# Attention over 32 memories and a SwiGLU block: memory values multiplied into the gate and value weights, attention with memories on partitions, engines ordered by the program

## The chip, the cores and the metric

The kernel runs on one core of one Trainium2 chip. The time is the device time of one execution in microseconds. The kernel before has a median of 433.32 us over three runs (431.91 to 434.16). A core has TensorE (matrix products into PSUM), VectorE, ScalarE (functions and copies), GpSimd (called POOL in the profile) and SyncE (SP, which issues transfers); 16 DMA engines move data between HBM and the on-chip memory SBUF. GpSimd issues transfers too, and those alone can change the type on the way.

## The reference

There are 8 batches, 8 heads, 576 positions, 64 numbers per head and 32 memories. For each batch and head, with `a` a softmax over the 32 memories of `phi`:

```python
k_m = einsum('bhsm,bhsd->bhmd', a, k)      # 32 memory keys of 64 numbers
v_m = einsum('bhsm,bhsd->bhmd', a, v)      # 32 memory values
```

`a` is `exp(phi - max over positions)` divided by its sum over positions; the sum runs over the 576 positions, for each memory. Then

```python
attn = softmax(q @ k_m.T / sqrt(64))       # over the 32 memories
x    = attn @ v_m                          # heads side by side: 4608 tokens x 512
out  = (silu(x @ w_gate) * (x @ w_val)) @ w_out
```

`w_gate` and `w_val` are 512 x 1536, `w_out` is 1536 x 512. Inputs and output are float32; the products are made in bfloat16 with float32 sums.

For one batch, `x @ w_gate` is the sum over heads of `attn_h @ (v_m_h @ w_gate_h)`, where `w_gate_h` are the 64 rows that belong to the head. The inner product has 8 x 32 = 256 rows, and so the product with `attn` has a contraction of 256 where `x @ w_gate` has 512.

## The kernel before, in words

A position s of a head lies on partition p = s // 6, column j = s % 6, with 96 partitions; the transposes put the 576 positions of a batch in the order (j, p), and the output's view `out_r` undoes it.

`attention_pair(b, a)` treats two heads. It loads phi by SyncE (L101) and q, k, v by GpSimd with a cast to bfloat16 (L105, L109, L113), six pieces of 256 bytes for each partition and head, adds columns of ones (L117), and takes exp of phi on ScalarE (L120). Six matmuls (L129, 258 columns: k and v of two heads and two columns of ones) give the memories with their sums. VectorE takes the reciprocals (L142), ScalarE scales into the two blocks of a block-diagonal `t_bkv` (L145), whose zeros GpSimd writes (L125). TensorE transposes the keys and q (L153, L155), VectorE copies them to SBUF (L162), six matmuls make the scores with positions on partitions (L166). ScalarE takes exp (L175), VectorE sums over memories, inverts and multiplies (L177 to L181). After the `yield` comes the back half: transposes of the weights of attention (L191), their copy (L198), and the product with the memory values (L202, L206), which ScalarE copies into X (L209, L210): 128 features of a pair of heads on partitions, 4608 tokens.

`ffn_chunk(c)` treats 512 tokens. For each of 12 blocks of 128 of the 1536 hidden features it runs four matmuls for the gate (L234) and four for the value (L242), each with 128 rows of contraction and 512 columns; ScalarE takes Tanh of half the gate (L250), VectorE makes two products (L252, L256). Then four tiles of 128 tokens: 12 matmuls each (L265), a copy on ScalarE (L273) and the transfer out (L275).

Weights come by SyncE as float32 and are cast by VectorE (L76, L77). The loops run over batches and pairs of heads; the back half of a pair is issued after the front half of the next, and a chunk as soon as its tokens are there. The order on each engine is not the order of the program: a planner places instructions by priority and by when their inputs are due, so that the profile shows attention of the next batch between the matmuls of a chunk.

Of the kernel before, what the change touches and what calls it, by code (L numbers as in the profile page):

```python
# [10 lines left out]
FP32 = mybir.dt.float32  # L12
# [4 lines left out]
def kernel(  # L17
# [10 lines left out]
):  # L28
    nc = tc.nc
    AF = mybir.ActivationFunctionType  # L30
    ALU = mybir.AluOpType
    AXL = mybir.AxisListType
# [4 lines left out]
    NT = out.shape[0]  # L37
    P, J = 96, 6
    KVC = 2 * (2 * D + 1)
    sm_scale = 1.0 / math.sqrt(D)  # L40

    n_pairs = H // 2
    N_CI = DM // 128
    N_FJ = DF // 128
    TCH = 512
    N_TC = NT // TCH

    consts = ctx.enter_context(tc.tile_pool(name="consts", bufs=1))
    bridge = ctx.enter_context(tc.tile_pool(name="bridge", bufs=1))
    wpool = ctx.enter_context(tc.tile_pool(name="wpool", bufs=1))  # L50
    wstage = ctx.enter_context(tc.tile_pool(name="wstage", bufs=3))

    att_sb = ctx.enter_context(tc.tile_pool(name="att_sb", bufs=3))
    ffn_sb = ctx.enter_context(tc.tile_pool(name="ffn_sb", bufs=2))
    ps = ctx.enter_context(tc.tile_pool(name="ps", bufs=1, space=bass.MemoryType.PSUM))

    ident = consts.tile([128, 128], BF16, tag="ident", name="ident")
    make_identity(nc, ident)

    Xs = [bridge.tile([128, NT], BF16, tag=f"X{i}", name=f"X{i}") for i in range(4)]  # L60

    WG = [wpool.tile([128, DF], BF16, tag=f"WG{i}", name=f"WG{i}") for i in range(N_CI)]
    WV = [wpool.tile([128, DF], BF16, tag=f"WV{i}", name=f"WV{i}") for i in range(N_CI)]
    WO = [wpool.tile([128, DM], BF16, tag=f"WO{i}", name=f"WO{i}") for i in range(N_FJ)]

    weight_jobs = []

    def _make_wjob(dst, src_ap, big, idx):
        def run():
            st = wstage.tile(  # L70
                [128, DF if big else DM],
                FP32,
                tag="wst_big" if big else "wst_small",
                name=f"wst{idx}",
            )
            nc.sync.dma_start(out=st, in_=src_ap)  # L76
            nc.vector.tensor_copy(out=dst, in_=st)  # L77

        return run

    _wi = 0
    for i in range(N_CI):
        weight_jobs.append(_make_wjob(WG[i], moe_w_gate[128 * i:128 * (i + 1), :], True, _wi))
        _wi += 1
    for i in range(N_CI):
        weight_jobs.append(_make_wjob(WV[i], moe_w_val[128 * i:128 * (i + 1), :], True, _wi))
        _wi += 1
# [263 lines left out]
```

## Time and profile before

| what | value |
|---|---|
| median of the runs | 433.32 us |
| span of the profiled execution | 430.0 us |
| between span and median | 3.3 us |
| TensorE busy | 377.2 us (88%) |
| VectorE busy | 229.4 us (53%) |
| ScalarE busy | 159.3 us (37%) |
| GpSimd busy | 155.3 us (36%) |
| moved by DMA | 38.16 MB, of it 14.17 MB by GpSimd's queue |
| first matmul | at 20.70 us |

No time of its own is given for the profiled execution beside its span; the median is that of three runs without a profile. The page divides the span into 40 equal slices and gives each engine a digit of tenths. Groups of instructions are given as busy time, mean time of one and idle time before them. Matmuls are pipelined, so the mean of one is longer than the distance between two; the distance is read from the timeline.

### The profile page before, as it was taken

How to read it: one execution, taken by the hardware profiler on the slowest of the kernel's cores; microseconds unless marked ns; L12 is line 12 of the kernel's file. 1: busy time of each engine (PE TensorE's matmuls, PEld its weight loads, DVE VectorE, ACT ScalarE, POOL GpSimd, SP SyncE). 2: the span in 40 equal slices, each digit the busy share in tenths (PEclk: the TensorE clock that was granted, in tenths of full speed). 3: DMA queues.
4: the chain of work that ended last, by engine and by line, in shares of the span. 5: the costliest groups of instructions: out<-in, count | busy, mean ns of one | idle time of the engine just before them, and what ended most of it. 6: DMA issues, size and time to landing. Idle time of an engine off the chain costs nothing.

```text
span 430.0 us, 6163 instructions
## 1 busy us (share of the span) xinstructions
PE 377.2 (88%) x2160; PEld 180.0 (42%) x2160; DVE 229.4 (53%) x460; ACT 159.3 (37%) x337; POOL 155.3 (36%) x262
## 2 busy tenths in 40 slices
PE   0036667999999999999999999999999999999995
PEld 0023333444444444444444444444444444444442
DVE  1136534780678067807780777077707770871760
ACT  1012333532553255335533553355334533332321
POOL 7068558750763076307621772176300000000000
PEclk9999955999999999999999999999999999999999
DMA  9999999992996299639963995398630003003003
GB/s 253 320 239 112 230 161 102 99 69 75 110 95 41 75 116 91 41 84 103 93 40 98 102 89 34 94 94 51 41 98 0 3 2 98 0 2 98 2 1 96
DMA packets 129502, 38.16 MB, mean 89 GB/s; under 512 B 116160, under 2 KB 122304, under 8 KB 129472
## 3 DMA queue, kind: packets, MB, share of 16 engines
q0 software_dynamic: 113664, 14.17, 53.7%
q1 hardware_dynamic: 15808, 23.60, 19.5%
q8 instruction: 17, 0.28, 0.3%
q14 instruction: 13, 0.11, 0.1%
HBM read 42.47 MB, written 9.44 MB: 121 GB/s over the span
## 4 chain that ended last, share of the span: by engine, by line
PE 74%; DMA 13%; POOL 6%; ACT 3%; issue 3%; DVE 0%; POOLq 0%; ACTq 0%; DVEq 0%
PE p_oo L265 22%; PE p_g L234 20%; PE p_v L242 19%; DMA t_kvb<-in_v_dram 13%; PE p_kvS L129 4%; PE p_aT L191 2%; POOL t_kvb L109 2%; POOL t_qb L105 2%; PE p_kqT L155 2%; PE p_sc L166 2%; PE p_o L202 2%; ACT t_T L250 1%; ACT t_bkv L145 1%; POOL t_kvb L113 1%; PE p_kqT L153 1%
## 5 line engine op out<-in xcount | busy, mean ns | idle before, releaser
L234 PE MATMUL p_g<-X,WG 128*128 128x512 bf16 x432 | 121.1, 385 | 0.6 <-ACT X L209 0.6
L242 PE MATMUL p_v<-X,WV 128*128 128x512 bf16 x432 | 119.3, 386 | 0.8 <-DVE t_B L252 0.8
L250 ACT ACTIVATE t_T<-p_g 128x512 bf16<-128x512 f32 x108 | 64.3, 595 | 88.2 <-PE p_g L234 82.7
L252 DVE SCALAR_TENSOR_TENSOR t_B<-t_T,p_v 128x512 bf16<-128x512 bf16 x108 | 74.0, 685 | 41.9 <-PE p_v L242 32.8
L265 PE MATMUL p_oo<-WO,t_h 128*128 128x512 bf16 x432 | 94.7, 379 | 0.0
L109 POOL DMA_DIRECT2D t_kvb<-in_k_dram x64 | 46.7, 730 | 80.8 <-PE p_kvS L129 75.1
L256 DVE SCALAR_TENSOR_TENSOR t_h<-t_B,p_g 128x512 bf16<-128x512 bf16 x108 | 73.2, 678 | 2.3
L265 PEld LDWEIGHTS <-t_h 128*128 128x128 bf16 x432 | 42.3, 98 | 50.9
L242 PEld LDWEIGHTS <-WV 128*128 128x128 bf16 x432 | 40.5, 99 | 48.2 <-issue 4.8
L234 PEld LDWEIGHTS <-WG 128*128 128x128 bf16 x432 | 38.3, 98 | 46.2 <-issue 8.9
L142 DVE RECIPROCAL t_rS<-p_kvS 32x1 f32<-32x1 f32 x64 | 10.1, 157 | 84.0 <-PE p_kvS L129 72.4
L129 PE MATMUL p_kvS<-t_kvb,t_ephi 96*64 96x258 bf16 x192 | 31.1, 304 | 24.7 <-POOL t_kvb L117 24.6
L273 ACT COPY t_o<-p_oo 128x512 f32<-128x512 f32 x36 | 21.1, 585 | 80.2 <-PE p_oo L265 80.2
L105 POOL DMA_DIRECT2D t_qb<-in_q_dram x64 | 48.5, 761 | 2.6 <-issue 2.6
L113 POOL DMA_DIRECT2D t_kvb<-in_v_dram x64 | 47.4, 741 | 2.9 <-issue 1.5
L145 ACT ACTIVATE t_bkv<-p_kvS,t_rS 32x128 bf16<-32x128 f32 x64 | 22.6, 353 | 37.6 <-DVE t_rS L142 32.7
L129 PEld LDWEIGHTS <-t_ephi 96*64 96x64 bf16 x192 | 20.5, 119 | 35.2 <-issue 33.5
L117 POOL MEMSET t_kvb<- 96x12 bf16 x32 | 4.8, 149 | 63.8 <-DMA t_kvb<-in_v_dram 63.7
L175 ACT ACTIVATE t_att<-p_sc 96x384 bf16<-96x384 f32 x32 | 15.5, 484 | 32.0 <-PE p_sc L166 31.9
L209 ACT CAST X<-p_o 128x512 bf16<-128x512 f32 x32 | 18.7, 584 | 18.8 <-PE p_o L206 18.8
L198 DVE COPY t_aT<-p_aT 64x576 bf16<-64x576 bf16 x32 | 14.3, 446 | 21.3 <-PE p_aT L191 21.3
L162 DVE COPY t_kqT<-p_kqT 128x640 bf16<-128x640 bf16 x32 | 15.7, 489 | 17.3 <-PE p_kqT L155 17.3
(28 smaller groups left out, 204.5 us busy)
## 6 DMA issues: line engine op xcount, KB each, us to landing
t_phi<-in_phi_dram SPq DMA_DIRECT2D x64, 72.0 KB, 2.8
t_qb<-in_q_dram POOLq DMA_DIRECT2D x64, 72.0 KB, 3.4
t_kvb<-in_k_dram POOLq DMA_DIRECT2D x64, 72.0 KB, 3.5
t_kvb<-in_v_dram POOLq DMA_DIRECT2D x64, 72.0 KB, 3.6
out_dram<-t_o SPq DMA_DIRECT2D x24, 192.0 KB, 2.3
wst<-in_moe_w_gate_dram SPq DMA_DIRECT2D x4, 768.0 KB, 7.1
wst<-in_moe_w_val_dram SPq DMA_DIRECT2D x4, 768.0 KB, 7.1
wst<-in_moe_w_out_dram SPq DMA_DIRECT2D x12, 256.0 KB, 5.3
```

What stands on the lines that cost most here:

```text
L105: nc.gpsimd.dma_start(out=t_qb[:, :, hh, :], in_=q[b, h].rearrange("(p j) d -> p j d", p=P),)
L109: nc.gpsimd.dma_start(out=kvb_heads[:, hh, :, 0:D], in_=k[b, h].rearrange("(p j) d -> p j d", p=P),)
L113: nc.gpsimd.dma_start(out=kvb_heads[:, hh, :, D:2 * D], in_=v[b, h].rearrange("(p j) d -> p j d", p=P),)
L129: nc.tensor.matmul(p_kvS, lhsT=t_ephi[:, j], rhs=t_kvb[:, j], start=(j == 0), stop=(j == J - 1),)
L145: nc.scalar.activation(out=bkv_blk[rows, :, D * hh:D * hh + D], in_=p_kvS[rows, off:off + 2 * D], func=AF.Copy, scale=t_rS[rows, :],)
L234: nc.tensor.matmul(p_g, lhsT=WG[i][:, 128 * jf:128 * (jf + 1)], rhs=Xs[i][:, cols], start=(i == 0), stop=(i == N_CI - 1),)
L242: nc.tensor.matmul(p_v, lhsT=WV[i][:, 128 * jf:128 * (jf + 1)], rhs=Xs[i][:, cols], start=(i == 0), stop=(i == N_CI - 1),)
L250: nc.scalar.activation(out=t_T, in_=p_g, func=AF.Tanh, scale=0.5)
L252: nc.vector.scalar_tensor_tensor(out=t_B, in0=t_T, scalar=1.0, in1=p_v, op0=ALU.add, op1=ALU.mult)
L256: nc.vector.scalar_tensor_tensor(out=t_h, in0=t_B, scalar=0.5, in1=p_g, op0=ALU.mult, op1=ALU.mult)
L265: nc.tensor.matmul(p_oo, lhsT=hts[jf][:, 128 * u:128 * (u + 1)], rhs=WO[jf], start=(jf == 0), stop=(jf == N_FJ - 1),)
L273: nc.scalar.copy(out=t_o, in_=p_oo)
```

## The change

The kernel is written anew. What it does:

- Every engine runs its instructions in the order in which the program issues them (`manual_schedule`).
- phi, q, k and v are loaded for a whole batch in one transfer each: eight heads, pieces of 1536 bytes (768 for phi). k and v come by GpSimd with a cast; q comes by SyncE as float32 and GpSimd casts it (`cast_q`). Weights come by GpSimd with a cast, in six pieces (`load_w`) and three (`load_wo`).
- `kv_group(b, g)` makes the memories of two pairs of heads: the pairs write partitions 0 to 63 and 64 to 127 of one PSUM tile. The sums are matmuls with one column of ones. VectorE scales and masks them into block-diagonal tiles of 128 x 128, `kv_T` transposes keys and values.
- `scores(b, g)` puts memories on partitions and positions on columns: 128 memories (four heads) x 288 positions a half. `z_norm` sums over the 32 memories of a head with a matrix of ones (`bones`), takes 1/Z as exp(-ln Z) on ScalarE, and VectorE multiplies.
- `u_step` multiplies the memory values of two pairs of heads with 512 columns of a weight: U, 128 memories x 512 features, copied to bfloat16 by ScalarE or VectorE. There are 12 a batch.
- `gv_slot(b, s)` makes 128 hidden features for 288 tokens: two matmuls for the gate, two for the value, Silu on ScalarE, one product on VectorE, which is issued one slot late. There are 24 a batch.
- The output projection works on tiles of 128 tokens over two batches; its matmuls are issued one at a time as fill.
- `window(b)` issues scores and normalisation of a batch with up to three output tiles between; `interleave` puts the rest of the output tiles and the next batch's attention between the slots.

```diff
...
+    ctx.enter_context(tc.manual_schedule())
...
+    def load_kv(b):
+        t = inp.tile([P, 2, H, J * D], BF16, tag="kv", name="t_kv")
+        nc.gpsimd.dma_start(out=t[:, 0], in_=k[b].rearrange("h (p j) d -> p h (j d)", p=P))
+        nc.gpsimd.dma_start(out=t[:, 1], in_=v[b].rearrange("h (p j) d -> p h (j d)", p=P))
...
+    def cast_q(b):
+        t = inp.tile([P, J, H, D], BF16, tag="q", bufs=1, name="t_q")
+        nc.gpsimd.tensor_copy(out=t.rearrange("p j h d -> p h j d"), in_=qf.pop(b))
...
+    def kv_group(b, g):
+        pk = ps.tile([128, 2 * 2 * D + 1], FP32, tag="s", name="p_kv")
...
+        for j in range(J):
+            for pp in range(2):
+                pr = 2 * g + pp
+                nc.tensor.matmul(
+                    pk[64 * pp:64 * pp + 64, 0:4 * D],
+                    lhsT=te[:, j, 2 * pr:2 * pr + 2],
+                    rhs=tk[:, :, 2 * pr:2 * pr + 2, j * D:(j + 1) * D],
...
+        r = att.tile([128, 1], FP32, tag="rS", name="t_rS")
+        nc.vector.reciprocal(out=r, in_=pk[:, 4 * D:4 * D + 1])
+        t = att.tile([128, 2, 128], BF16, tag=f"bkv{g}", name="t_bkv")
+        for w in range(2):
+            nc.vector.scalar_tensor_tensor(
+                out=t[:, w], in0=pk[:, 128 * w:128 * w + 128], scalar=r, in1=mask,
+                op0=ALU.mult, op1=ALU.mult,
             )
...
+    def scores(b, g):
+        p = ps.tile([128, 2, 512], FP32, tag="gv", name="p_sc")
+        for hf in range(2):
+            for pp in range(2):
+                nc.tensor.matmul(
+                    p[64 * pp:64 * pp + 64, hf, 0:HALF],
+                    lhsT=kvTs[b][:, 0, g, 64 * pp:64 * pp + 64],
+                    rhs=qTs[b, 2 * g + pp][:, hf * HALF:(hf + 1) * HALF],
...
+        nc.scalar.activation(out=e, in_=p[:, :, 0:HALF], func=AF.Exp, scale=sm_scale)
...
+    def z_norm(b, g):
+        p = ps.tile([128, 2, 512], FP32, tag="gv", name="p_z")
+        e = es.pop((b, g))
+        for hf in range(2):
+            nc.tensor.matmul(p[:, hf, 0:HALF], lhsT=bones, rhs=e[:, hf], start=True, stop=True)
...
+        nc.scalar.activation(out=lz, in_=p[:, :, 0:HALF], func=AF.Ln)
+        rz = att.tile([128, 2, HALF], FP32, tag="rz", bufs=1, name="t_rz")
+        nc.scalar.activation(out=rz, in_=lz, func=AF.Exp, scale=-1.0)
+        a = att.tile([128, 2, HALF], BF16, tag=f"A{g}", name="t_A")
+        nc.vector.tensor_tensor(out=a, in0=e, in1=rz, op=ALU.mult)
...
+    def u_step(b, which, c, g, eng):
+        p = ps.tile([128, CH], FP32, tag="s", name="p_u")
+        for pp in range(2):
             nc.tensor.matmul(
+                p[64 * pp:64 * pp + 64, :],
+                lhsT=kvTs[b][:, 1, g, 64 * pp:64 * pp + 64],
+                rhs=W[which, c][:, 2 * g + pp],
...
+        t = upool.tile([128, CH], BF16, tag=f"U{which}{c}{g}", name="t_U")
+        if eng == "a":
+            nc.scalar.copy(out=t, in_=p)
+        else:
+            nc.vector.tensor_copy(out=t, in_=p)
...
+    def gv_slot(b, s):
...
+        p = ps.tile([128, 2, 512], FP32, tag="gv", name="p_gv")
+        for which in range(2):
+            for g in range(NG):
+                nc.tensor.matmul(
+                    p[:, which, 0:HALF],
+                    lhsT=Us[b, which, c, g][:, 128 * r:128 * (r + 1)],
+                    rhs=atts[b, g][:, hf],
+                    start=(g == 0),
+                    stop=(g == NG - 1),
+                )
+        sg = work.tile([128, HALF], BF16, tag="sg", name="t_sg")
+        nc.scalar.activation(out=sg, in_=p[:, 0, 0:HALF], func=AF.Silu)
+        flush_mul()
...
+        def mul():
+            nc.vector.tensor_tensor(out=dst, in0=sg, in1=p[:, 1, 0:HALF], op=ALU.mult)
...
+    def out_list(b):
+        if b < 0:
+            return []
+        c = b // 2
+        tiles = range(0, 4) if b % 2 == 0 else range(4, 9)
+        res = []
+        for n, u in enumerate(tiles):
+            res += out_units(c, u, "v" if n < 3 else "a")
+        return res
+
+    def next_attention(b):
+
+        items = [(700, lambda g=g: kv_group(b, g)) for g in range(NG)]
+        items += [(330, lambda pr=pr: q_T(b, pr)) for pr in range(2)]
+        items += [(250, lambda: kv_T(b))]
+        items += [(330, lambda pr=pr: q_T(b, pr)) for pr in range(2, 4)]
+        n = 0
+        for c in range(NCH):
+            for which in range(2):
+                for g in range(NG):
+                    eng = "v" if n % 5 in (1, 3) else "a"
...
+                        (230, lambda c=c, which=which, g=g, eng=eng: u_step(b, which, c, g, eng))
...
+    def interleave(slots, fill):
+        total = sum(x[0] for x in fill)
+        acc, i = 0.0, 0
+        for s, fn in enumerate(slots):
+            fn()
+            while i < len(fill) and acc + fill[i][0] / 2 <= total * (s + 1) / len(slots):
+                acc += fill[i][0]
+                fill[i][1]()
+                i += 1
...
+    def window(b, fill):
+        nc.scalar.preload_act_table_set("natural_log_exp_and_others")
+        for g in range(NG):
+            scores(b, g)
+        if b + 1 < B:
+            phi_exp(b + 1)
+        cut = len(fill) // 3
+        for x in fill[:cut]:
+            x[1]()
+        for g in range(NG):
+            z_norm(b, g)
+        for x in fill[cut:]:
+            x[1]()
...
+    load_phi(0)
+    load_q(0)
+    load_phi(1)
+    make_identity(nc, ident)
...
+    load_kv(0)
+    for c in range(NCH):
+        for which in range(2):
+            load_w(which, c)
+    load_kv(1)
+    for c in range(3):
+        load_wo(c)
+    cast_q(0)
+    load_q(1)
...
     for b in range(B):
...
+        if b + 2 < B:
+            load_phi(b + 2)
+            load_kv(b + 2)
+        o = out_list(b - 1)
+        window(b, o[:36])
+        rest = o[36:]
+        slots = [lambda s=s: gv_slot(b, s) for s in range(2 * NJF)]
+        nxt = next_attention(b + 1) if b + 1 < B else []
+        if b + 1 < B:
+            cast_q(b + 1)
+        if b + 2 < B:
+            load_q(b + 2)
+        if b == 0:
+            for c in range(NCH):
+                for x in u0[4 * c:4 * c + 4]:
+                    x[1]()
+                for s in slots[8 * c:8 * c + 8]:
+                    s()
+            for x in nxt:
+                x[1]()
+        else:
+            interleave(slots, rest + nxt)
+        flush_mul()
+    for x in out_list(B - 1):
+        x[1]()
...
```

PSUM has eight banks: the pairs `gv` (slots, scores, Z) take two buffers of two banks, `s` (memories, transposes, U) two of one, `o` (output tiles) two of one. The fill units carry a weight each (the first number); they set only where a unit stands between the slots.

More of the change, by code (lines that the diff above doesn't have):

```diff
@@ L2 @@
 import math
-from collections import deque
 from contextlib import ExitStack
@@ L31 @@
     ALU = mybir.AluOpType
-    AXL = mybir.AxisListType
     B, H, S, D = q.shape
@@ L157, in attention_pair @@
[L157 removed]
+                pq[:, P * j:P * (j + 1)],
+                qs[b][:, j, 2 * pr:2 * pr + 2],
                 ident[0:P, 0:P],
             )
[L161 to L165 removed]
+        t = att.tile([128, S], BF16, tag=f"qT{pr}", name="t_qT")
+        nc.vector.tensor_copy(out=t, in_=pq)
```

373 lines of the change are left out of this document (147 added, 226 removed).

## The prediction

> **What bounds the kernel now.** I read the page's first two parts, then the chain of waits, then TensorE's order of time, to see which stage loses what. The page's head:
>
> ```profile
> span 430.0 us, 6163 instructions
> PE 377.2 (88%) x2160; PEld 180.0 (42%) x2160; DVE 229.4 (53%) x460; ACT 159.3 (37%) x337; POOL 155.3 (36%) x262
> PE   0036667999999999999999999999999999999995
> DMA  9999999992996299639963995398630003003003
> PE 74%; DMA 13%; POOL 6%; ACT 3%; issue 3%; DVE 0%; POOLq 0%; ACTq 0%; DVEq 0%
> ```
>
> A slice is 10.75 us. TensorE is idle for two slices and at six tenths for the next five, while the DMA engines are full; after that it is always busy. So there are two stages: a start bound by transfers, then a long stretch bound by matmuls. The profiled span is 430.0 us and the median of the runs 433.32 us, so 3.3 us lie around the span; I sum against the span and add them.
>
> The groups of instructions (busy us, mean ns), the chain (start, us) and the timeline (start, us):
>
> ```profile
> L234 PE MATMUL p_g<-X,WG 128*128 128x512 bf16 x432 | 121.1, 385 | 0.6 <-ACT X L209 0.6
> L242 PE MATMUL p_v<-X,WV 128*128 128x512 bf16 x432 | 119.3, 386 | 0.8 <-DVE t_B L252 0.8
> L265 PE MATMUL p_oo<-WO,t_h 128*128 128x512 bf16 x432 | 94.7, 379 | 0.0
> 95.80 10.36 PE p_oo L265 x48
> 138.43 10.36 PE p_oo L265 x48
> 148.19 0.59 PE L265 MATMUL p_oo<-WO,t_h 128*128 128x512 bf16 x2
> 148.72 0.85 PE L129 MATMUL p_kvS<-t_kvb,t_ephi 96*64 96x258 bf16 x6
> 149.51 0.82 PE L234 MATMUL p_g<-X,WG 128*128 128x512 bf16 x3
> 151.26 0.43 PE L155 MATMUL p_kqT<-ident,t_qb 96*128 96x96 bf16 x6
> 151.52 0.60 PE L234 MATMUL p_g<-X,WG 128*128 128x512 bf16 x2
> ```
>
> Means of 385 ns overlap; the price is the distance. 48 matmuls of 512 columns in 10.36 us: 0.216 us each, 0.42 ns a column. The 258-column L129 keeps that rate: 0.79 us from its start to L234's, less 6 x 0.109, leaves 0.14 us. L265 ends streaming at 148.19 + 2 x 0.216 = 148.62, and L129 starts at 148.72: 0.10 us. So going into the 64-column arrangement and out of it costs about 0.24 us. The 128-wide transposes L155 take (151.52 - 151.26)/6 = 0.043 us each, so loading 128 columns of weights fits in 0.043 us and doesn't bound a 288-column matmul (0.121 us).
>
> The method on the old kernel: between the two L265 blocks lie 42.63 us. In them are 144 matmuls of 512 columns (31.1 us) and four pairs of attention at some 2.5 us with their switches (10.0 us): 41.1 us, so 1.5 us (4%) are waits.
>
> **What the change does to TensorE, per batch.** Gate and value: before, a batch needs 864 x 0.216 / 8 = 23.3 us of p_g and p_v. After, 24 slots of four matmuls with 288 columns: 96 x 0.121 = 11.7 us. This is the gain: 11.6 us a batch, 93 us in all. Output projection: unchanged, 54 x 0.216 = 11.7 us. Added: 12 U steps, each a pair of 64-column matmuls of 512 columns. K/V: 24 matmuls of 256 columns and 24 of one column; q transposes 24 x 0.043 = 1.0 us (as before); four transposes of 128 (0.2 us); scores, 8 of 288 columns; the sum over memories, 4 of 288 (0.5 us).
>
> The two matmuls of a pair in U, K/V and scores write the two halves of the partitions, hence use the two halves of the columns. No row shows two at once. Bounds from the 0.216 us row: at most one after the other (U 5.2, K/V 2.6 + 24 x 0.05 = 3.8, scores 1.0: 10.0 us), at least side by side (half, 5.0 us). I take the lower end: the 0.24 us round trip around L129 shows that the array is rearranged for 64 columns, so that the other half is free. Switches: scores, two K/V groups and the U steps in some seven lots, 10 x 0.24 = 2.4 us.
>
> Sum side by side: 11.7 + 11.7 + 5.0 + 1.0 + 0.2 + 0.5 + 2.4 = 32.5 us, serial 37.5 us.
>
> The Trainium skill ("TensorEngine Tiling (Array Packing)", section Tiling Modes) says that tiles work in parallel and that changing the mode drains TensorE. The second rule speaks against U steps strewn among 128-wide slots, and the 0.10 and 0.14 us above agree with it; for the first, "TensorE: Matmul & The Clock Gate", Part 3, gives 2.38 times for three column tiles, by which a pair would be somewhat dearer than half: an estimate by that page is some 6 us a batch for these three items in place of 5.0. No run here shows it yet.
>
> **The other engines per batch.** The rows for their prices:
>
> ```profile
> L250 ACT ACTIVATE t_T<-p_g 128x512 bf16<-128x512 f32 x108 | 64.3, 595 | 88.2 <-PE p_g L234 82.7
> L175 ACT ACTIVATE t_att<-p_sc 96x384 bf16<-96x384 f32 x32 | 15.5, 484 | 32.0 <-PE p_sc L166 31.9
> L273 ACT COPY t_o<-p_oo 128x512 f32<-128x512 f32 x36 | 21.1, 585 | 80.2 <-PE p_oo L265 80.2
> L120 ACT ACT_TABLE_LOAD x1 | 1.3, 1283 | 3.3 <-DMA t_phi<-in_phi_dram 3.3
> L256 DVE SCALAR_TENSOR_TENSOR t_h<-t_B,p_g 128x512 bf16<-128x512 bf16 x108 | 73.2, 678 | 2.3
> L198 DVE COPY t_aT<-p_aT 64x576 bf16<-64x576 bf16 x32 | 14.3, 446 | 21.3 <-PE p_aT L191 21.3
> ```
>
> ScalarE: 0.87 ns an element between L175 and L250, so a Silu of 288 is 0.40 us, x24 = 9.6; exponentials, Ln and Exp over 576 about 0.65 us, x6 = 3.9; exp of phi over 1536 elements 1.5; seven U copies at 0.585 = 4.1; 1.5 output copies 0.9; two table loads 2.6: 22.6 us. VectorE: 24 products of 288 from PSUM at 1.04 ns an element and 0.15 us (from 678 for 512) = 0.45, x24 = 10.8; five U copies and three output copies of 512 at some 0.66 = 5.3; four q copies 1.8; two normalisations 1.5; the masks, reciprocals and the memory copy 1.9: 21.3 us. Both fit under 32.5 us. What before they did (Tanh, two products of 512 a tile) also fitted, so their saving is worth nothing by itself.
>
> Where they can stall TensorE: a slot's PSUM pair comes free after Silu and product; two pairs exist. From the end of the gate's matmuls to a free pair: 0.40 + 0.45 + 0.2 = 1.05 us, and TensorE meanwhile has the value matmuls, a slot and two fills of some 0.45 us, 1.6 us: covered. In the last third of a batch's slots the U steps come two a slot and put a copy in front of Silu or product on one engine; I allow 1 us. The window: the table load and the two exponentials run under one output tile (12 x 0.216 = 2.6 us), Ln to product under two more (5.2 us): covered, where batch 0 has no output tile and pays the chain of 7.3 us. The Silu table load (1.28 us) waits with the first Silu: 0.5 us a window; the scores wait for the last slot's product: 0.5 us. Together 2.5 us: **35 us** a batch, against 42.6.
>
> **The start.** Transfers now:
>
> ```profile
> q0 software_dynamic: 113664, 14.17, 53.7%
> q1 hardware_dynamic: 15808, 23.60, 19.5%
> 9.72 0.72 POOL L113 DMA_DIRECT2D t_kvb<-in_v_dram  x1 [1.32 <-DMA t_qb<-in_q_dram]
> 20.70 1.45 PE L129 MATMUL p_kvS<-t_kvb,t_ephi 96*64 96x258 bf16 x6 [20.70 <-POOL t_kvb L117]
> L125 POOL MEMSET t_bkv<- 64x256 bf16 x32 | 10.1, 315 | 25.5 <-PE p_o L206 25.3 <-POOL t_kvb L117 0.2
> ```
>
> The queue of GpSimd has 113,664 packets of 256 bytes read, 0.537 x 430 x 16 / 113,664 = 32.5 ns each; SyncE's queue 84.9 ns for 1.5 KB, 281 GB/s on 16 engines. The change turns q, k and v from 256-byte pieces into pieces of 1.5 KB, and weights into 2 KB pieces. At SyncE's price a batch needs 4.1 MB in and 1.2 MB out, 19 us of 35: hidden. In the old row at 9.72 the ninth GpSimd transfer waits for the first one. By that, after: two for K/V, six weights, then two for the next K/V and three for the output weights, each waiting for one eight earlier, and only behind them GpSimd casts q of batch 0. The last needs 2.4 MB (phi, q, phi) + 2.4 (k, v) + 3.1 (three weight pieces) = 7.9 MB, 28 us, plus 2 of landing. The cast of 3072 elements: L125's 315 ns for 256 is at most 1.2 ns an element, 3.8 us; 5 with its strided write. With the transposes and copies the scores of batch 0 start at 37 us. Behind the waiting cast on GpSimd stands only the next K/V load.
>
> **Sum.** Start 37. Batch 0: window 7.3, table load 1.3, 24 slots without fill, each bound by the hand-over of 1.3 us for two (15.6), two breaks for U steps 3.4, batch 1's attention alone 10: 37.6. Six batches at 35: 210. Batch 7: window 10.3, slots 15.6, table 1.3: 27. Tail: five tiles, 60 x 0.216 = 13, last product, copy and landing 3.5: 16.5. Span 328.1, with 3.3 around it 331.4; I say **331 us**. Its own range is 312 (no stalls, start at 30) to 345.
>
> **Rivals.** (1) The pairs run one after the other, as every row of this trace does: 5 us a batch on seven periods that TensorE fills, less some where VectorE waits hide it: 331 + 27 = 358 us. Chance 0.22. (2) Cast transfers cost by the byte as the old queue: 32.5 ns for 256 bytes is 195 ns for 1.5 KB; K/V 18.7 us a batch, weights 3072 x 260 / 16 = 50 us; the output weights come at about 112 us, where window 1 needs them at 75. Batch 0 is some 30 us longer: 361. For it the 32.5 ns row, against it SyncE's. 0.12. (3) The hand-over decides: where a copy stands in front of Silu and product alike, 0.245 + 0.585 + 0.40 + 0.66 + 0.45 + 0.2 = 2.54 us for two slots, 30.5 for 24, a batch of 41: 118 + 246 + 3 = 367. Against it: at most two copies a slot, and only in a third of the slots. 0.12. (4) The other side: ScalarE's tables. If Copy isn't served by the table that Silu loads, each of the 8.5 copies a batch costs two loads, 17 x 1.28 = 22 us, exposed through two PSUM pairs: 35 + 22 = 57 us a batch, 118 + 342 + 3 = 463. It decides from 52 us a batch ((430 - 118)/6), 13 exposed loads. Against it: the old profile has one load for Exp, Tanh and copies together. 0.04. That the contraction isn't halved can't be: each slot has four matmuls, counted above.
>
> **The numbers.** Forecast 0.50, rivals 0.22, 0.12, 0.12, 0.04. The range of 308 to 366 takes the first, the serial pairs and the transfers whole. A change under 0.5% can't be told from none here: faster 0.95, same 0.01, slower 0.04.
>
> **What would show it.** 768 gate and value matmuls of 288 columns, 0.121 us apart; a U pair in 0.22 us (0.43 would be rival 1); 35 us from window to window; some 17 table loads; the first scores at 37 us, behind GpSimd's cast. Above 345 us without rival 1, a wait that I have not seen stands in the slots.

## The result and the profile after

The changed kernel takes 335.24 us (median of four runs, 334.37 to 338.31), the kernel before on the same chip 433.74 us. The ratio is 0.775, with a 95% interval of 0.771 to 0.779. Executions come in a faster and a slower state, and here and below times are compared in the faster one. The forecast was 331, within 308 to 366: right in kind, 4 us short. But the parts of the sum miss by more than the sum does, and the same wait is behind the two largest misses.

From the page of the changed kernel: its head, the engines by slices and the chain of waits.

```profile
span 332.5 us, 5356 instructions
...
PE 272.5 (82%) x2076; PEld 159.3 (48%) x2096; DVE 165.1 (50%) x371; ACT 177.5 (53%) x333; POOL 41.8 (13%) x39
...
PE   0044587878989899989998999989898999898894
...
q1 hardware_dynamic: 18304, 23.60, 28.5%
q0 software_dynamic: 17296, 14.16, 27.9%
...
PE 64%; DVE 15%; DMA 7%; ACT 7%; issue 3%; POOL 2%; another core or an unknown queue 1%; SPq 0%; ACTq 0%; POOLq 0%
...
L248 PE MATMUL p_gv<-t_A,t_U 128*128 128x288 bf16 x768 | 126.4, 288 | 14.1 <-DVE t_h L262 13.0
L218 PE MATMUL p_u<-W,t_kvT 128*64 128x512 bf16 x192 | 34.3, 403 | 6.2 <-ACT t_U L227 4.2
```

TensorE's busy time falls by 104.7 us, from 377.2 to 272.5. The gate and value products explain 93.3 of it: 864 matmuls at 0.216 us (186.6) have become 768 at 0.1215 us (93.3). Its idle time rises, from 52.8 us to 60.0 (some 1 us of this stands for 20 matmuls without a record, 2076 of 2096), and the slices no longer stand at 9: in the chain of waits VectorE has gone from 0% to 15% and ScalarE from 3% to 7%. L248 shows where: 13.0 us of idle time ahead of the slots, ended by the product `t_h`. A slot waits for VectorE.

The view of stretches, cut where a batch's first scores start (us of the stretch, then busy us of TensorE, weight loads, VectorE, ScalarE and GpSimd, then the granted clock, the DMA share and GB/s):

```profile
0.00:32.69 32.69, 6.17 (x76) 5.63 (x77) 4.20 (x21) 4.05 (x3) 14.90 (x22) 1.00 1.12 205
32.69:75.55 42.86, 31.92 (x233) 16.42 (x234) 21.85 (x46) 23.71 (x46) 7.02 (x4) 1.00 1.07 203
75.55:285.68 210.13, 196.59 (x1559) 116.73 (x1572) 121.50 (x270) 131.33 (x249) 19.84 (x13) 1.00 0.46 97
285.68:332.50 46.82, 37.79 (x213) 20.51 (x215) 17.54 (x34) 18.42 (x37) 0.00 (x0) 0.98 0.20 51
```

These are the start, batch 0, batches 1 to 6, and the last batch with its output tiles. In the six middle batches TensorE is busy for 94% of the time, in batch 0 for 74%, in the last for 81%. The clock of 1.00 doesn't hold for the first 44 us: the trace has no record of the clock before 44.1 us, and the matmuls themselves show about half the speed. Two U matmuls take 0.64 us at 39.35 in the timeline below, where four take 0.62 at 209.16; matmuls of 288 columns start 0.24 us apart up to 44.06 and 0.12 us apart from there. Against the sum:

| term | forecast | measured | difference |
|---|---|---|---|
| start | 37 | 32.69 | -4.3 |
| batch 0 | 37.6 | 42.86 | +5.3 |
| batches 1 to 6 | 210 | 210.13 | +0.1 |
| batch 7 and tail | 43.5 | 46.82 | +3.3 |
| span | 328.1 | 332.5 | +4.4 |

From the timeline (start, us of the group, engine, line; in brackets the idle time before it and what ended it). The parts are, in order, the start of the kernel with the first window, the last third of batch 4 with the scores of batch 5, and the last slots of batch 7:

```profile
26.26 0.74 POOL L110 DMA_DIRECT2D WO<-in_moe_w_out_dram  x1 [1.85 <-DMA W<-in_moe_w_gate_dram]
27.00 2.75 POOL L93 CAST t_q<-t_qf 96x3072 bf16<-96x3072 f32 x1
29.81 1.14 PE L173 MATMUL p_q<-ident,t_q 96*128 96x96 bf16 x12 [7.82 <-POOL t_q L93]
32.69 1.26 PE L188 MATMUL p_sc<-t_qT,t_kvT 128*64 128x288 bf16 x8
39.35 0.64 PE L218 MATMUL p_u<-W,t_kvT 128*64 128x512 bf16 x2 [3.03 <-ACT t_U L227]
...
208.58 0.65 PE L248 MATMUL p_gv<-t_A,t_U 128*128 128x288 bf16 x4 [0.15 <-DVE t_h L262]
209.16 0.62 PE L218 MATMUL p_u<-W,t_kvT 128*64 128x512 bf16 x4
209.72 0.66 PE L248 MATMUL p_gv<-t_A,t_U 128*128 128x288 bf16 x4
210.31 0.67 PE L218 MATMUL p_u<-W,t_kvT 128*64 128x512 bf16 x4
...
216.26 1.28 ACT L348 ACT_TABLE_LOAD   x1
216.98 0.44 PE L188 MATMUL p_sc<-t_qT,t_kvT 128*64 128x288 bf16 x4 [0.90 <-DVE t_h L262]
...
312.03 0.65 PE L248 MATMUL p_gv<-t_A,t_U 128*128 128x288 bf16 x4 [0.28 <-DVE t_h L262]
312.72 0.41 ACT L256 ACTIVATE t_sg<-p_gv 128x288 bf16<-128x288 f32 x1 [0.52 <-DVE t_h L262]
313.16 0.46 DVE L262 TENSOR_TENSOR t_h<-t_sg,p_gv 128x288 bf16<-128x288 bf16 x1 [0.47 <-ACT t_sg L256]
313.67 0.65 PE L248 MATMUL p_gv<-t_A,t_U 128*128 128x288 bf16 x4 [0.28 <-DVE t_h L262]
```

**Side by side.** From 209.16 to 209.72 two U steps are done, four matmuls of 512 columns, in 0.56 us with the switch. One after the other they would take 4 x 0.216 = 0.86 us. So the two halves run at once: half of 0.86 is 0.43, and 0.13 remains for the switch back. The way in is 209.16 - 208.58 less the slot's 4 x 0.121, 0.09 us. Both ways 0.22, as forecast (0.24).

**The hand-over.** The slot at 312.03 holds four matmuls of 0.121 us, two for the gate, then two for the value. Silu reads the gate's half alone, and so the forecast let it start after 0.245 us. It starts at 312.72, when all four have ended. Then 0.41 us of Silu, 0.46 us of product, and at 313.67 the pair of banks is free for the slot after next. That is 1.64 us for two slots where the sum had 1.3. Between these starts TensorE has two slots and one output matmul, 4 x 0.245 + 0.216 = 1.2 us of work, and idles for the rest.

### The profile page after: what moved, and what is told of

Read it like the earlier page. It is cut to its first block, busy times and chain, and to the rows that moved or that the text cites. A ratio compares the mean times of both kernels' runs of the same rounds, so it can differ in the third digit from the quotient of the medians.

```text
span 332.5 us, 5356 instructions
## 1 busy us (share of the span) xinstructions
PE 272.5 (82%) x2076; PEld 159.3 (48%) x2096; DVE 165.1 (50%) x371; ACT 177.5 (53%) x333; POOL 41.8 (13%) x39
## 3 DMA queue, kind: packets, MB, share of 16 engines
q0 software_dynamic: 17296, 14.16, 27.9%
## 4 chain that ended last, share of the span: by engine, by line
PE 64%; DVE 15%; DMA 7%; ACT 7%; issue 3%; POOL 2%; another core or an unknown queue 1%; SPq 0%; ACTq 0%; POOLq 0%
PE p_oo L286 24%; PE p_gv L248 24%; DVE t_h L262 8%; PE p_u L218 8%; DMA W<-in_moe_w_gate_dram 6%; ACT t_sg L256 4%; PE p_kv L134 3%; DVE t_qT L179 2%; DVE t_U L229 2%; DVE t_bkv L155 2%; PE p_q L173 2%; PE p_sc L188 1%; PE p_z L203 1%; ACT t_U L227 1%; POOL t_q L93 1%
## 5 line engine op out<-in xcount | busy, mean ns | idle before, releaser
L248 PE MATMUL p_gv<-t_A,t_U 128*128 128x288 bf16 x768 | 126.4, 288 | 14.1 <-DVE t_h L262 13.0
L256 ACT ACTIVATE t_sg<-p_gv 128x288 bf16<-128x288 f32 x192 | 79.0, 411 | 93.9 <-PE p_gv L248 60.9
L262 DVE TENSOR_TENSOR t_h<-t_sg,p_gv 128x288 bf16<-128x288 bf16 x192 | 86.2, 451 | 44.7 <-ACT t_sg L256 44.5
L248 PEld LDWEIGHTS <-t_U 128*128 128x128 bf16 x768 | 70.5, 98 | 60.5 <-issue 31.2
L218 PE MATMUL p_u<-W,t_kvT 128*64 128x512 bf16 x192 | 34.3, 403 | 6.2 <-ACT t_U L227 4.2
L227 ACT CAST t_U<-p_u 128x512 bf16<-128x512 f32 x56 | 32.1, 586 | 9.9 <-PE p_u L218 8.8
L229 DVE CAST t_U<-p_u 128x512 bf16<-128x512 f32 x40 | 27.7, 691 | 18.0 <-PE p_u L218 16.8
L298 DVE COPY t_o<-p_oo 128x512 f32<-128x512 f32 x24 | 16.5, 689 | 35.7 <-PE p_oo L286 35.7
L134 PE MATMUL p_kv<-t_kv,t_ephi 96*64 96x256 bf16 x192 | 14.8, 294 | 18.6 <-DMA t_kv<-in_v_dram 18.6
L93 POOL CAST t_q<-t_qf 96x3072 bf16<-96x3072 f32 x8 | 22.0, 2745 | 52.5 <-PE p_q L173 30.4
L134 PEld LDWEIGHTS <-t_ephi 96*64 96x64 bf16 x192 | 10.2, 117 | 21.7 <-issue 21.7
L173 PEld LDWEIGHTS <-t_q 96*128 96x128 bf16 x192 | 11.9, 102 | 10.2 <-POOL t_q L93 7.9
```

What stands on the lines that cost most here:

```text
L93: nc.gpsimd.tensor_copy(out=t.rearrange("p j h d -> p h j d"), in_=qf.pop(b))
L134: nc.tensor.matmul(pk[64 * pp:64 * pp + 64, 0:4 * D], lhsT=te[:, j, 2 * pr:2 * pr + 2], rhs=tk[:, :, 2 * pr:2 * pr + 2, j * D:(j + 1) * D] ...
L173: nc.tensor.transpose(pq[:, P * j:P * (j + 1)], qs[b][:, j, 2 * pr:2 * pr + 2], ident[0:P, 0:P],)
L218: nc.tensor.matmul(p[64 * pp:64 * pp + 64, :], lhsT=kvTs[b][:, 1, g, 64 * pp:64 * pp + 64], rhs=W[which, c][:, 2 * g + pp], start=True, st ...
L227: nc.scalar.copy(out=t, in_=p)
L229: nc.vector.tensor_copy(out=t, in_=p)
```

## The experiments

The theory after this reading: the kernel consists of a start that waits for a cast, a middle that TensorE fills, and two ends that wait for the hand-over. The Silu waits for the value matmuls because gate and value share a PSUM tile. The runs take these one by one, then join what helped. Each time is a median; the ratio is to the kernel before on the same chip (433.1 to 434.6 us).

### What the shorter contraction is worth

Each slot's four matmuls are issued twice, which gives back the number of gate and value matmuls of a contraction twice as long.

```diff
-        for which in range(2):
+        for which in (0, 0, 1, 1):
```

> Each slot makes its gate and its value product twice over (eight matmuls of 288 columns in place of four; the second writes the same numbers). Theory (TensorE bounds, and the halved contraction is worth its 11.7 us a batch): six middle batches 11 us longer each, batches 0 and 7, where the hand-over bounds, go from 1.64 to 2.13 us for two slots, 5.9 us each: 412 to 422 us. Rival (another engine bounds the slots): under 390 us.

408.5 us, ratio 0.943 [0.940, 0.945]: 73 us more. The added matmuls are 768 x 0.1215 = 93.3 us; a middle batch grows by 10.0 us of 11.7, batch 0 by 7.6. The rest of them falls into time in which the changed kernel idles: the wait of slots for `t_h` shrinks from 13.0 us to 0.5. It is a little less than was expected. So of the 98 us that the change brings, 73 hang on the halved contraction, and some 25 on the rest of the rewriting.

### Two 64-column halves against one full width

The memory values of a pair are padded with zeros to 128 columns (a tile `Vz`), and a U step becomes two full-width matmuls that accumulate: no switch, no parallel halves.

```diff
...
-                p[64 * pp:64 * pp + 64, :],
-                lhsT=kvTs[b][:, 1, g, 64 * pp:64 * pp + 64],
+                p,
+                lhsT=Vz[:, g, pp],
...
-                start=True,
-                stop=True,
+                start=(pp == 0),
+                stop=(pp == 1),
```

> The two matmuls of a U pair are made one after the other at full width: the transposed memory values lie in a tile with zeros in the other pair's columns, so that both matmuls write all 128 partitions and add up. Nothing else changes but two more VectorE copies a batch. Theory (a pair runs side by side in the changed kernel): a pair of 512 columns goes from 0.22 to 0.43 us, 12 x 0.21 = 2.5 us a batch, less six switches of arrangement at 0.13 us: 1.7 us a batch, six to seven of them on TensorE's path: 345 to 349 us. Rival (the pairs already run one after the other): nothing is added and the switches go: 328 to 335 us.

343.55 us, ratio 0.794 [0.790, 0.798]; a middle batch takes 1.08 us more, less than the 1.7 expected. From its timeline:

```profile
214.66 1.03 PE L224 MATMUL p_u<-W,t_Vz 128*128 128x512 bf16 x4
215.52 0.65 PE L254 MATMUL p_gv<-t_A,t_U 128*128 128x288 bf16 x4
216.01 1.05 PE L224 MATMUL p_u<-W,t_Vz 128*128 128x512 bf16 x4
```

Four full-width matmuls take 215.52 - 214.66 = 0.86 us, and the slot after them 0.49 us: 1.35 us a round, with nothing lost between. The changed kernel's round is 1.14 us (208.58 to 209.72). So of the 0.43 us that the halves save in a round, the two switches take back half.

The Trainium skill ("TensorEngine Tiling (Array Packing)", Tiling Modes) states both: tiles work independently, and changing the mode drains TensorE. Both runs agree, and put the price at 0.22 us a round trip.

### When Silu may start

Two runs ask what the Silu waits for. The first issues it between the gate's and the value's matmuls, in the same PSUM tile; the second gives gate and value a tile of one bank each (`scores` and `z_norm` use the same two tiles, with the exponentials and logarithms in halves).

```diff
         for which in range(2):
             for g in range(NG):
                 nc.tensor.matmul(
...
+            if which == 0:
+                sg = work.tile([128, HALF], BF16, tag="sg", name="t_sg")
+                nc.scalar.activation(out=sg, in_=p[:, 0, 0:HALF], func=AF.Silu)
-        sg = work.tile([128, HALF], BF16, tag="sg", name="t_sg")
-        nc.scalar.activation(out=sg, in_=p[:, 0, 0:HALF], func=AF.Silu)
```

> Silu is issued between the gate's and the value's two matmuls; every engine keeps its own order. Theory (Silu waits for all four matmuls of a slot, because it is issued behind them): it starts 0.24 us earlier after the slot's start, two slots of the hand-over go from 1.64 to 1.40 us, 24 slots of batch 0 and of batch 7 are 2.9 us shorter each, the batches between 0.5 to 1 us: 324 to 331 us. Rival (the wait is for the shared PSUM tile, by the whole tile): the value's matmuls then wait for Silu as well, two slots take over 2 us: 350 us or more. Second rival (the wait is not what bounds): 335 us.

447.42 us (three other runs took 460.05 to 461.25), worse than the kernel before with 433.62. The rival was right. From the list of waits (total us, times, longest) and the timeline of the run of 461.25 us:

```profile
PE p_gv L248 <- ACT t_sg L257: 102.5, 192, 0.9
```

```profile
200.87 0.41 PE L248 MATMUL p_gv<-t_A,t_U 128*128 128x288 bf16 x2 [0.64 <-ACT t_sg L257]
```

All 192 slots stop in the middle: the value's matmuls, into the other bank of the same tile, wait until Silu has read the gate's. So order is kept by whole tile here, not by what is read and written in it.

```diff
...
-        p = ps.tile([128, 2, 512], FP32, tag="gv", name="p_gv")
-        for which in range(2):
+        pg = ps.tile([128, 512], FP32, tag="g", name="p_g")
+        pv = ps.tile([128, 512], FP32, tag="v", name="p_v")
+        for which, p in enumerate((pg, pv)):
...
-        nc.scalar.activation(out=sg, in_=p[:, 0, 0:HALF], func=AF.Silu)
+        nc.scalar.activation(out=sg, in_=pg[:, 0:HALF], func=AF.Silu)
```

> Gate and value get a PSUM tile of one bank each in place of one tile of two banks; exp and Ln of a batch's window are taken in two halves (six more ScalarE instructions a batch, some 0.2 us each, under the output tiles). Theory (Silu waits for the tile): Silu starts 0.24 us earlier, two slots of hand-over 1.40 us; 324 to 331 us. Rival (the tile is not the cause): 335 us, or up to 338 with the added instructions exposed in batch 0.

318.06 us, ratio 0.736 [0.731, 0.740]: 17 us less than the changed kernel, more than was expected. From its timeline, the first slots of batch 7:

```profile
286.72 0.41 PE L251 MATMUL p_g<-t_A,t_U 128*128 128x288 bf16 x2
286.96 0.41 PE L251 MATMUL p_v<-t_A,t_U 128*128 128x288 bf16 x2
287.16 0.41 ACT L259 ACTIVATE t_sg<-p_g 128x288 bf16<-128x288 f32 x1 [1.50 <-PE p_g L251]
287.42 0.41 PE L251 MATMUL p_g<-t_A,t_U 128*128 128x288 bf16 x2
287.67 0.41 PE L251 MATMUL p_v<-t_A,t_U 128*128 128x288 bf16 x2
```

The gate's two matmuls end at 287.13 and Silu starts at 287.16, while the value's run. The slots of batch 7 follow each other without a wait for `t_h`, 0.60 us apart with their output matmuls, where they were 0.82. In the profiled execution, which at 320.56 us was the longest of the four and had half the clock from 65.5 to 75.8 us, batch 0 has lost 3.1 us, a middle batch 0.95 and the last 5.0. The edit does two things: Silu starts earlier, and the gate's bank is free after Silu, not after the product. Their shares were not separated.

### What ends the start

The cast of q is moved ahead of five transfers on GpSimd's queue, those of batch 1's k and v and of the output weights.

```diff
+    cast_q(0)
     load_kv(1)
     for c in range(3):
         load_wo(c)
-    cast_q(0)
```

> The cast of batch 0's q is issued on GpSimd ahead of the transfers of batch 1's k and v and of the output weights; nothing else moves. Theory (the start waits for the cast, which stands behind transfers that each wait for one eight earlier): the cast ends before 18.6 us, where k and v of batch 0 are there; scores of batch 0 at about 24 us in place of 32.7; the first two weight pieces are there at 24, so the rest moves with it: 326 to 329 us. Rival (the start is bound by the bytes: the weights or batch 1's k and v are late next): under 3 us, 332 to 336 us.

327.98 us, ratio 0.759 [0.753, 0.764]. From its timeline:

```profile
12.41 2.74 POOL L93 CAST t_q<-t_qf 96x3072 bf16<-96x3072 f32 x1 [4.77 <-DMA t_qf<-in_q_dram]
...
25.71 1.26 PE L188 MATMUL p_sc<-t_qT,t_kvT 128*64 128x288 bf16 x8
```

The scores start 7.0 us earlier and the time falls by 7.3. What released the cast before was the last of the queued transfers that must wait for an earlier one (26.26 in the changed kernel's timeline); now it is q itself.

### What the windows need

No output matmuls between scores, Z and the slots; all of them go between the slots.

```diff
-        window(b, o[:36])
-        rest = o[36:]
+        window(b, [])
+        rest = o
```

> No output tiles stand in the windows; they all go between the slots. Theory (the three tiles cover a chain of some 8 to 9 us from the scores to the first slot): the window keeps that length, and 7.8 us of matmuls come to the slots of batches 1 to 6; batch 7 has room for them: six times 6 to 7 us, 370 to 380 us. Rival (the chain is shorter, or the slots have room for three more tiles): under 355 us.

388.81 us, ratio 0.897 [0.895, 0.900]: 8.6 us a middle batch, more than the 6 to 7 expected. From its stretches (the granted clock is the column after the five engines) and its timeline, in the window of batch 5:

```profile
252.00:253.00 1.00, 0.44 (x4) 0.23 (x4) 0.36 (x1) 0.99 (x2) 0.00 (x0) 1.00 1.11 222
253.00:254.00 1.00, 0.67 (x3) 0.31 (x3) 0.00 (x0) 1.00 (x3) 0.00 (x0) 0.73 1.09 221
254.00:255.00 1.00, 0.49 (x2) 0.15 (x1) 0.00 (x0) 1.00 (x1) 0.00 (x0) 0.50 1.03 198
...
262.00:263.00 1.00, 1.00 (x3) 0.30 (x2) 0.46 (x1) 0.39 (x1) 0.00 (x0) 0.50 0.00 0
263.00:264.00 1.00, 1.00 (x6) 0.65 (x5) 0.00 (x0) 0.00 (x0) 0.00 (x0) 0.65 0.00 0
264.00:265.00 1.00, 1.00 (x9) 0.60 (x7) 0.46 (x1) 0.41 (x1) 0.00 (x0) 1.00 0.00 0
```

```profile
252.41 0.44 PE L188 MATMUL p_sc<-t_qT,t_kvT 128*64 128x288 bf16 x4 [0.90 <-DVE t_h L262]
253.31 1.18 PE L203 MATMUL p_z<-t_E,bones 128*128 128x288 bf16 x4 [0.46 <-ACT t_E L196]
257.26 0.40 PE L248 MATMUL p_gv<-t_A,t_U 128*128 128x288 bf16 x1 [2.77 <-DVE t_A L209]
258.83 0.88 PE L248 MATMUL p_gv<-t_A,t_U 128*128 128x288 bf16 x3 [1.17 <-DVE t_A L209]
```

The fill is worth two things. It covers the chain through ScalarE and VectorE, visible here as 0.46 + 2.77 + 1.17 us of idle time. And it keeps the clock: from about 253.5 to 263.7 TensorE is granted half of it. From 258.8 on TensorE has work, so some 4.9 us are worked at half speed and 2.4 us lost, about what the batch takes beyond the expectation; that last step is worked out, not measured by a run of its own.

The Trainium skill ("TensorE: Matmul & The Clock Gate", What's actually happening) has the clock halved after an idle window of about 3.4 us that runs freely. The half agrees with the 0.50, and the window with the times of the changes in this run: 219.33, 253.46 and 263.70 are ten and three times 3.41 us apart. The idleness doesn't agree: in the 3.41 us before the fall (250.05 to 253.46) TensorE was busy for 1.62 us, with no gap longer than 0.90. In the changed kernel a stretch as long with 2.44 us of busy time (71.41 to 74.82) left the clock at 1.00. So a stretch that is idle in part was enough here; how large the part must be isn't settled by these runs.

### Whether the tables cost anything

In place of Silu stands Exp, which the table for exponentials and logarithms serves; the output is another.

```diff
-        nc.scalar.activation(out=sg, in_=p[:, 0, 0:HALF], func=AF.Silu)
+        nc.scalar.activation(out=sg, in_=p[:, 0, 0:HALF], func=AF.Exp)
```

> Silu is replaced by Exp, which lies in the table that is already loaded, so the output is another; all but the first table loads go. Theory (after the trace: both loads of a batch lie under output tiles): 333 to 336 us. Rival (the prediction's term of 0.5 us a window, and the load before the scores' exp on the path as well): 4 to 14 us less, 321 to 331 us.

334.89 us, ratio 0.775 [0.770, 0.781]: no difference, with eight loads fewer. The loads of the changed kernel stand under other work: that at 216.26 holds the exponentials back to 217.55, while the second scores wait for VectorE until 216.98 and output matmuls run from 217.57.

### The order by hand, and the tables again

The planner is given the same program.

```diff
-    ctx.enter_context(tc.manual_schedule())
```

> The one line that fixes the order of the program on every engine is taken out of the changed kernel, so that the planner orders it as it ordered the kernel before. Theory (the shorter contraction and TensorE's work make the gain; waits are some 2 us a batch in either order): 325 to 352 us. Rival (the order written out is what covers the waits): 370 us or more.

361.4 us (two runs, 359.31 and 363.58), ratio 0.834 [0.828, 0.840]: 26 us more, between the two expectations. The profile has 56 table loads where the changed kernel has 17, and so a second run keeps the order by hand and only leaves out the two lines that load a table ahead of time.

```diff
-        nc.scalar.preload_act_table_set("natural_log_exp_and_others")
...
-    nc.scalar.preload_act_table_set("natural_log_exp_and_others")
```

> The order written out is kept; only the lines that load the table with exp and ln together are taken out, so that exp and Ln come from tables of their own, as in the run under the planner (its trace has 14 loads in front of Ln and 14 in front of the exp behind it). Theory (those loads are what the planner's order lost): a batch has five loads in place of two, the window's chain is 4 to 5 us longer and the output tiles no longer cover it: 355 to 372 us. Rival (the planner lost by its order of the matmuls): 335 to 345 us.

369.28 us, ratio 0.853 [0.850, 0.857]. From its groups by form (busy us, mean ns):

```profile
L205 ACT ACT_TABLE_LOAD x16 | 20.5, 1283 | 0.3
L207 ACT ACT_TABLE_LOAD x16 | 20.5, 1283 | 0.3
L256 ACT ACT_TABLE_LOAD x8 | 10.3, 1283 | 0.1
L196 ACT ACT_TABLE_LOAD x7 | 9.0, 1283 | 0.1
```

Ln (L205) and the Exp after it (L207) now each load a table of their own, both times in a window, where the two preloads chose one that has both: 48 loads in all. They stand in the chain from the scores to the slots; a middle batch takes 39.4 us, 4.4 more than 35.0. This alone costs 34 us, more than the 26 of the planner. In both traces the slots wait for `t_A`, the end of that chain: 19.6 us here and 27.2 under the planner, where the changed kernel has no such wait. The clock suffers too: over the six middle batches its mean is 0.97 here, 0.94 under the planner and 1.00 in the changed kernel. So what the hand-written order brings here over the planner needs no better order of matmuls; that the planner's order without the added loads would be as fast is likely, but wasn't run.

The Trainium skill ("ScalarE: Activation LUTs", What ACT_TABLE_LOAD costs) gives a load 1283 ns, as every row here has, and a drain of about 1380 ns beside it. The timeline of this run shows no such drain: a load at 165.53 and Ln at 166.82, a load at 167.49 and Exp at 168.79.

### Transfers in small pieces

k and v are loaded for each head by itself, 16 transfers a batch in pieces of 256 bytes in place of two with pieces of 1536.

```diff
-        nc.gpsimd.dma_start(out=t[:, 0], in_=k[b].rearrange("h (p j) d -> p h (j d)", p=P))
-        nc.gpsimd.dma_start(out=t[:, 1], in_=v[b].rearrange("h (p j) d -> p h (j d)", p=P))
+        for h in range(H):
+            nc.gpsimd.dma_start(out=t[:, h, :, 0:D], in_=k[b, h].rearrange("(p j) d -> p j d", p=P))
+            nc.gpsimd.dma_start(out=t[:, h, :, D:2 * D], in_=v[b, h].rearrange("(p j) d -> p j d", p=P))
```

> k and v are loaded as before the change: one transfer per head and tensor (16 a batch in place of two), pieces of 256 bytes. Everything else is the changed kernel. Theory (1.5 KB pieces shorten the start, the middle has room): at 32.5 ns for a piece a batch's k and v take 18.7 us of the DMA engines in place of 4 to 8; scores of batch 0 at 45 to 52 us in place of 32.7, the middle the same or up to 2 us a batch longer where q, phi and the output are late: 347 to 366 us. Rival (the pieces don't matter): 334 to 339 us.

356.80 us, ratio 0.820 [0.818, 0.822]. The first scores start at 55.60, 22.9 us later, and the middle batches take what they took (34.69 us from 98.45 to 133.14). Loading a batch in one transfer thus matters for the start alone: there, 32 transfers of k and v stand ahead of the cast of q on GpSimd's queue, which comes at 49.86 where it came at 27.00. The edit makes the pieces smaller and the transfers more at once; what each does by itself wasn't run, but issuing 32 transfers at 0.73 us takes 23 us on that queue, where four took 3.

### Joined

The first version joins the two PSUM tiles, the early cast, batch 1's attention between the slots of batch 0 (which the changed kernel runs after them, alone), and moves an output tile from batch 6 into batch 7.

```diff
...
-            for c in range(NCH):
-                for x in u0[4 * c:4 * c + 4]:
-                    x[1]()
-                for s in slots[8 * c:8 * c + 8]:
-                    s()
-            for x in nxt:
+            for x in u0[:4]:
                 x[1]()
+            interleave(slots[:8], u0[4:8])
+            interleave(slots[8:16], nxt[:5] + u0[8:])
+            interleave(slots[16:], nxt[5:])
```

> Gate and value in tiles of their own, the early cast of batch 0's q, batch 1's attention between batch 0's slots instead of behind them, and one output tile moved from batch 6 to batch 7's slots and one from batch 7's window. Theory (the gains of the first two add, 17 and 7 us; the attention of batch 1, some 12 us alone, takes some 7 us between slots of 0.55 us that leave TensorE little room, so 4 to 6 us; the moved tiles fill batch 7's slots, which leave nothing since they no longer wait, so 0 to 3 us): 300 to 308 us. Rival (with an early start the weights or batch 1's k and v are late and hold the first batch): 311 to 316 us.

315.31 us, ratio 0.725 [0.723, 0.727]. The rival's time came out: batch 0 takes 41.8 us, and k and v of batch 1 are late. TensorE's clock is at half besides, from 46.67 to 53.50, with 6.55 us of work in it; what each costs wasn't separated. From its timeline:

```profile
46.95 1.49 PE L134 MATMUL p_kv<-t_kv,t_ephi 96*64 96x256 bf16 x12 [5.46 <-DMA t_kv<-in_v_dram]
```

The moved tile brings nothing: against the two-tile run batch 6 is 1.6 us shorter (33.1 for 34.7) and the last 3.2 longer (45.0 for 41.8).

The second version leaves the tile where it was, issues q of batch 1 on GpSimd's queue behind batch 1's k and v, and puts batch 1's attention between the last six slots of batch 0. The edit is shown against the changed kernel.

```diff
...
+    cast_q(0)
     load_kv(1)
+    load_q(1, nc.gpsimd)
...
+            interleave(slots[:8], u0[4:8])
+            interleave(slots[8:16], u0[8:])
+            for s in slots[16:18]:
+                s()
+            interleave(slots[18:], nxt)
```

> As the joined kernel before it, but the output tiles of batches 6 and 7 stay where the change put them, q of batch 1 is loaded by GpSimd's queue behind batch 1's k and v (so that it doesn't run beside them), and batch 1's attention stands between the last six slots of batch 0. Theory (the joined kernel lost its gain because k and v of batch 1 came at 46.9 us, 5.5 us late, with q of batch 1 and the weights beside them, and because the moved tiles cost 1.6 us): k and v at 42 to 45 us, the scores of batch 1 at 58 to 62 us in place of 66.8: 305 to 311 us. Rival (the first 50 us are bound by bytes however they are ordered, or the attention in six slots is bound by the copies): 312 to 317 us.

311.27 us, ratio 0.717 [0.715, 0.718], 0.3 above what was expected, and the fastest version here: 24 us under the changed kernel. From its stretches:

```profile
0.00:27.44 27.44, 6.10 (x77) 5.55 (x77) 3.98 (x21) 4.05 (x3) 12.69 (x19) 1.00 1.09 209
27.44:64.50 37.06, 29.93 (x233) 16.05 (x234) 21.07 (x47) 23.21 (x49) 7.77 (x8) 0.91 1.22 223
64.50:267.98 203.48, 196.50 (x1574) 116.42 (x1572) 120.37 (x270) 133.07 (x273) 22.15 (x14) 1.00 0.51 107
267.98:310.00 42.02, 36.54 (x218) 20.73 (x214) 17.51 (x34) 18.77 (x40) 0.00 (x0) 1.00 0.22 57
```

Start 5.3 us shorter, batch 0 by 5.8, the middle by 6.7, the end by 4.8. In the middle TensorE is busy for 97%; most of what is left lies in the first 64 us.

## Why the prediction was right or wrong, step by step

- **What bounds the kernel, and the halved contraction: right.** TensorE filled the kernel before, and taking 93 us from it brought 73 (the doubled products). The distance of 0.121 us for 288 columns held.
- **Side by side, and the switches: right.** 0.56 us for two U steps, and 0.22 for both switches. The first rival is refuted. Its price was too high for a kernel that would be written for it: for U, 2.6 of its 5 us a batch, full-width steps, which switch nothing, cost 1.08 us.
- **A middle batch, 35 us: right, 35.02.** Its 32.5 us of work and 2.5 of waits measured 32.8 and 2.3, but not for the reasons given. The Silu table load, put at 0.5 us, cost nothing (Exp in its place changed nothing); the wait of the scores for the last product, put at 0.5, is 0.90.
- **The hand-over: the step that failed.** "From the end of the gate's matmuls to a free pair: 0.40 + 0.45 + 0.2 = 1.05 us" let Silu start behind the gate's matmuls. It starts behind the value's. That makes 1.64 us for two slots, not 1.3. Where slots stand bare, the 24 of batch 7 took 19.2 us (295.65 to 314.86) and not 15.6, and those of batch 0 20.2 beside the breaks for U. The diff has gate and value in one PSUM tile, and the step left that out: with a tile each, and Silu issued at the same place, Silu starts behind the gate's (287.16 in the two-tile run). In the middle batches it was called covered; the two-tile run is about 1 us a batch shorter there too, though that edit also frees the gate's bank sooner.
- **Batch 0, 37.6 us: 5.3 short.** Of it 4.6 lie in the slots: 1.1 in the first four, three of them at half the clock (40.84 to 45.20, 4.36 us where the hand-over alone gives 2 x 1.64), the rest by the hand-over; 0.3 in the two breaks for U (47.92 to 49.83 and 56.21 to 57.95, 3.65 for 3.4); 0.9 in the attention alone (10.9 for 10). The way from the scores to the first slot, with the first four U steps in it, took 8.2 us and not 8.6 (7.3 and the table load's 1.3): the load hid, but TensorE worked at half the speed, where the sum had the full one.
- **Batch 7 and the tail: 3.3 short.** 3.6 by the hand-over and 1.1 in the tail, less the 1.3 of a table load that wasn't exposed.
- **The start, 37 us: 4.3 too long.** The order was right: the cast stood behind a transfer that waits for an earlier one, and moving it brought 7.3 us. The sizes were off: the cast began at 27.00 and not at 30 (28 and 2 of landing), it takes 2.75 us, not 5, and from its end to the scores went 2.9 us, not 2.
- **Transfers by the byte (the second rival): refuted.** GpSimd's queue took 0.279 x 332.5 x 16 / 17,296 = 86 ns a packet of 1.5 to 2 KB, what SyncE's took before, not 195.
- **The hand-over decides (the third rival): half right.** Not by copies in front of Silu and product, and not in the middle, but in batches 0 and 7 it did decide.
- **Tables (the fourth rival): refuted for this kernel,** with 17 loads, as forecast. Its price was real: 31 loads more, without the preloads, cost 34 us.

So the total came out within 4 us because a start that was too long (4.3 us) paid for half of two ends that were too short (8.6 us). That these cancel is luck.

## What to carry to other kernels

Before a PSUM hand-over is priced, look at which tile the reader shares with instructions that it doesn't need: here two halves that are read at different times, given a tile each, were worth 17 us of 335. When an inner product is shortened, the work between a chain of other engines shrinks with it; look for the stretches without fill, since there the chain sets the time, and give them fill or a shorter chain. On a queue that both issues transfers and computes, put the computation ahead of every transfer that may have to wait.

## What the runs showed that was not expected

- A write into one bank of a two-bank tile waits for a read of the other bank: 192 waits, 102.5 us (Silu between the matmuls).
- Granted clock fell to 0.50 at about 253.5 us in the bare window of batch 5, after gaps of no more than 0.90 us, and stayed there for 10.2 us. In the 3.41 us before, TensorE had been busy for 1.62. What share decides isn't settled by these runs.
- A granted clock of 1.00 can stand where the trace has no record of it: up to 44.1 us the changed kernel's matmuls ran at half speed, which only their distances show.
- Leaving out two preloads of a table adds 31 loads of 1283 ns and 34 us; the planner added 39.
- An issue on GpSimd's queue takes about as long for a small transfer (0.73 us, k or v of one head) as for one eight times as large (0.79 us), so splitting k and v into 16 delays what stands behind them.
